# Attention visits in one piece from the fourth token block on, a third Gm buffer and a new order of issue

## The chip, the cores and the metric

The kernel runs on one core of a Trainium2 chip. The metric is the device time of one execution in microseconds (us). Before the change three runs took 610.43, 612.09 and 612.76 us, a median of 612.09. The profile is of one further execution, which took 611.65 us.

## The reference

The input passes through a decaying linear attention and then through two feed-forward layers of the same shape. Reduced to what matters:

```python
# attention: 4 batches, 8 heads, 768 steps, head size 32, state 16
cum = cumsum(log(clip(a, 1e-6, 1)))                  # within a chunk
M = (C @ B.T) * exp(cum_i - cum_j) * causal          # per head
y = M @ x + (C @ state) * exp(cum)
state = exp(cum_end) * state + (B * exp(cum_end - cum)).T @ x
x = y as 3072 tokens of 256
# layer 1, weights 256 x 2048 and 2048 x 256
h = x @ w_in;  g = h / (1 + exp(-h));  x = g @ w_out
# layer 2, the same shapes
h = x @ w_in;  g = P(h) / (Q(h) + 1e-6);  x = g @ w_out
# P of third degree; Q = 1 + |b0||h| + |b1|h^2
```

## The kernel before

The tokens are cut into 24 blocks of 128, six to a batch. For every block n the attention takes these steps. A DMA brings the block's x, B and C (`tok`, L561), and from block 3 on another brings decay factors (`Ee`, L579). GpSimd builds the masked decays `Gm` by four selects (L590) and scales B (L607). VectorE or GpSimd multiplies C with factors (L613), ScalarE or VectorE spreads it over pairs of heads (L618, L620), GpSimd scales it once more (L629). From block 9 on a copy of C and B is split into a high and a low part (`cf`, L647 and L651). TensorE makes C times B (tile `att`, input `tok` or `cf`); VectorE multiplies it with Gm into two tiles `M` (L700). TensorE then makes the output (from `M`, and from the state `S`) and the state's increment (`att<-tok`, 128 x 64), and VectorE masks and adds the increment (`um` L788, `S` L792). ScalarE writes the output rounded (`y1h`, L802), VectorE the rest (`y1l`, L805). The TensorE work of a block is its **visit**.

Both layers go through the 2048 hidden units in 16 slices f of 128. An **in-product** (tile `h`, in layer 2 also `b`) is six matmuls: high weight times high x, high times low, low times high, twice. An **out-product** (tile `acc`) is six matmuls on `gh` and `gl`, the activation's rounded part (L844, L846) and the rest (L850). Between the two stands ScalarE's activation (L888 in layer 1). Layer 1 goes through seven groups of blocks, of 2, 2, 4, 4, 4, 4 and 4; in the first two the activation stays in PSUM, so the in-product two slices on needs the buffer that `gl` frees. Layer 2 goes through six groups of 512 tokens.

The weights come as 64-bit floats, 512 KB for each slice and layer (`wraw`, L472, three buffers). ScalarE expands the upper word (`wv`, L489), VectorE shifts (L495) and joins the lower word (L497), which frees the buffer. ScalarE rounds (L513), and VectorE or GpSimd makes the rest, the **split** (L517). Layer 2's weights are prepared during layer 1, stored to DRAM (L529), and reloaded into a slice's place (L539) once its last layer-1 out-product is done.

All DMAs are issued by SP, in a single order. The order on every engine comes from a planner: `Plan.run` takes, of the operations that can start soonest by its cost table, the one with the smallest key, and some operations have a choice of engine. The keys come from the numbers in `K` (L31 to L69). 23 **fillers** (`acc<-T`, matmuls on zeros whose result is not used) have the last key of all and fall where the planner finds TensorE free. The order is fixed when the kernel is built; on the chip each engine works through its own list and waits where an input is not there.

`ALONE` (L79) says for which blocks C times B, output and increment are three operations of the planner; later visits are one operation that makes C times B of the next block, then the output, then the increment of this one. Before, that holds for blocks 0 to 4. `ring("Gm", 2, ...)` (L310) gives Gm two buffers.

Of the kernel before, what the change touches and what calls it, by code (L numbers as in the profile page):

```python
# [14 lines left out]
P = 128  # L15
B, H, S, D, N = 4, 8, 768, 32, 16
# [12 lines left out]
HALVED = 0  # L29
TAIL_FLEX = 1  # L30
K = dict(  # L31
    t0=-18.163,
    step0=2.86,
    lag1=43.503,
    fo1=10.942,
    fo2=4472.323,
    fol=32.531,
    tab=-80.822,
    lead=168.696,
    kt=-12.237,  # L40
    kq=-77.043,
    kl=20.552,
    kg=62.898,
    ks=777.795,
    warm=23,
    warm0=5.147,
    warmstep=0.414,
    late=46.508,
    tab0=-2757.678,
    bulk=-58.119,  # L50
    d0=-14.734,
    gap0=36.588,
    d2=-19.542,
    d3=2.257,
    early2=9.278,
    early=24.026,
    w2a=-1512.003,
    w2b=-160.848,
    w1=-1.707,
    w1step=-31.741,  # L60
    w1load=3869.872,
    tokload=-233.083,
    ahead=17.68,
    eps=0.031,
    step2=168.582,
    dT=[-64.27, 36.68, -1.66, 34.6, -29.6, -174.18, 35.5, -3.13, -9.78, 138.44, -41.72, -26.53],
    dD=[-124.33, -53.44, 1.94, -60.08, -128.23, 35.27, -89.78, -84.57],
    dW=[28.05, -44.69, -91.49, 180.41, 166.11, 92.54, 19.47, 34.68, 21.96, 122.42, 25.71, 20.72, -50.06, -0.22, -24.39, 76.24],
)  # L69
SET_LN_EXP, SET_SILU = 6, 18  # L70

# [4 lines left out]
C_DIF, C_REF, C_PAR, C_MASK, C_CUM, C_CEND = 0, 128, 134, 136, 200, 840  # L76
SW = 2 * D
IN_PSUM = 2
ALONE = 5  # L79
PARTS = 9  # L80


# [28 lines left out]
class Plan:  # L111
# [9 lines left out]
    def add(self, choices, key, deps=(), new=(), use=(), wr=(), rd=(), cols=0, after=0.0, big=True, soft=False):  # L121
        op = Op(choices, key, list(deps), list(new), list(use), wr, rd, cols, after, big, soft)
        self.ops.append(op)
        return op
# [91 lines left out]
def ssd_moe_moe_kernel(ctx: ExitStack, tc: tile.TileContext, tok, la_in, consts, w1, w2, ab, outT):  # L216
# [17 lines left out]
    def ring(tag, n, cols, dt=F32, space="SB"):  # L234
        rings[tag] = (Ring(n), n, cols, space)
# [71 lines left out]
    ring("cum", 1, C_CEND - C_CUM)  # L307
    ring("lab", 2, P)
    ring("Ee", 4, P + R5)
    ring("Gm", 2, H * P)  # L310
    ring("M", 3, 512)
    ring("S", 2, SW)
    ring("um", 1, SW)
# [396 lines left out]
    def cb_alone(n):  # L710
        t, T, d, o_cx = at[n][0], at[n][1], at[n][2], at[n][5]
        cb, f_cb = cb_part(n)
        o_cb = add({"PE": (0.61, f_cb)}, T + 2 * d, o_cx, new=[cb], use=[t], wr=range(4), cols=4 * DM, big=False)
        masked(n, cb, o_cb)


    def visit(n):
# [30 lines left out]
        y_len = 0.55 + (0.33 if pv else 0)  # L748
        if n < ALONE:
            o_y = add({"PE": (y_len, f_y)}, T + 5 * d, y_deps, new=[yb], use=y_use, wr=[0, 1], cols=P, big=False)  # L750
            if us:
                o_u = add({"PE": (0.21, f_u)}, T + 4 * d, [o_bw], new=[ub], use=[t], wr=[2], big=False)
            if n + 1 < min(NTB, ALONE + 1):
                cb_alone(n + 1)
# [415 lines left out]
```

## Time and profile before

| | |
|---|---|
| median of three runs | 612.09 us |
| the profiled execution | 611.65 us |
| its span, first to last instruction | 609.9 us |
| mean granted TensorE clock | 0.985 |
| busy: TensorE, VectorE, ScalarE, GpSimd | 597.7, 441.9, 401.2, 375.8 us |
| bytes moved by DMA | 47.30 MB |

The profile counts an engine as busy while it works on an instruction; waits on semaphores are idle time, and each is put down to what ended it. PE is TensorE, PEld its weight load, DVE VectorE, ACT ScalarE, POOL GpSimd, SPq the issue of DMAs by SP. The granted clock is a share of 2.4 GHz. The start of a stretch is counted from the first instruction.

### The profile page before, as it was taken

How to read it: one execution, taken by the hardware profiler on the slowest of the kernel's cores; microseconds unless marked ns; L12 is line 12 of the kernel's file. 1: busy time of each engine (PE TensorE's matmuls, PEld its weight loads, DVE VectorE, ACT ScalarE, POOL GpSimd, SP SyncE). 2: the span in 40 equal slices, each digit the busy share in tenths (PEclk: the TensorE clock that was granted, in tenths of full speed). 3: DMA queues.
4: the chain of work that ended last, by engine and by line, in shares of the span. 5: the costliest groups of instructions: out<-in, count | busy, mean ns of one | idle time of the engine just before them, and what ended most of it. 6: DMA issues, size and time to landing. Idle time of an engine off the chain costs nothing.

```text
span 609.9 us, 9980 instructions
## 1 busy us (share of the span) xinstructions
PE 597.7 (98%) x3501; PEld 478.6 (78%) x3505; DVE 441.9 (72%) x740; ACT 401.2 (66%) x782; POOL 375.8 (62%) x493
## 2 busy tenths in 40 slices
PE   7799999999999999999999999999999999999997
PEld 4478798887777777777888888888888788878875
DVE  5799988665344435432313899999999999999994
ACT  5678777554333333322335898989988988898893
POOL 5878846205344444222201599899889889889984
PEclk8599999999999999999999999999999999999999
DMA  7765778751111000000036600000000000000000
GB/s 258 227 199 209 234 250 286 243 200 37 46 28 36 23 21 27 1 2 1 1 104 199 250 0 1 36 1 1 35 1 2 34 1 1 35 1 1 35 2 34
DMA packets 18314, 47.30 MB, mean 78 GB/s; under 512 B 2136, under 2 KB 5336, under 8 KB 18264
## 3 DMA queue, kind: packets, MB, share of 16 engines
q1 hardware_dynamic: 18264, 46.67, 23.1%
q8 instruction: 27, 0.44, 0.3%
q14 instruction: 23, 0.19, 0.1%
HBM read 34.99 MB, written 11.67 MB: 77 GB/s over the span
## 4 chain that ended last, share of the span: by engine, by line
PE 88%; DVE 4%; DMA 4%; ACT 2%; issue 1%; SPq 0%; DVEq 0%; ACTq 0%
PE acc L280 42%; PE h L280 35%; PE b L280 7%; PE att L280 4%; DMA wraw<-in_w_dram 3%; DMA Ee<-dre 1%; DVE wv L497 1%; DVE w L517 1%; ACT wv L489 1%; DVE M L700 1%; DVE wv L495 0%; DVE gl L850 0%; ACT w L513 0%; DVE tok L613 0%; DVE y1l L805 0%
## 5 line engine op out<-in xcount | busy, mean ns | idle before, releaser
L280 PE MATMUL h<-y1h,w 128*128 128x512 f32 (+1 forms) x700 | 229.4, 377 | 2.3 <-DVE gl L850 1.9
L280 PE MATMUL acc<-gh,w 128*128 128x512 f32 (+1 forms) x832 | 213.1, 377 | 0.2 <-ACT gh L844 0.2
L280 PEld LDWEIGHTS acc<-gh,w 128*128 128x128 f32 x832 | 149.4, 188 | 30.6 <-POOL gh L846 0.4
L280 PEld LDWEIGHTS h<-y1h,w 128*128 128x128 f32 x700 | 129.7, 189 | 31.9 <-DVE gl L850 3.0
L850 DVE TENSOR_TENSOR gl<-T,gh 128x512 fp32r<-128x512 f32 x79 | 57.4, 727 | 116.0 <-POOL gh L846 84.8
L280 PE MATMUL h<-y1l,w 128*128 128x512 f32 (+1 forms) x350 | 130.8, 374 | 0.0
L850 POOL TENSOR_TENSOR gl<-g,gh 128x512 fp32r<-128x512 f32 x95 | 123.1, 1300 | 11.5 <-ACT gh L844 4.5
L280 PE MATMUL acc<-gl,w 128*128 128x512 f32 (+1 forms) x416 | 123.8, 378 | 0.0
L846 POOL TENSOR_SCALAR gh<-T 128x512 fp32r<-128x512 f32 x54 | 33.9, 627 | 137.2 <-ACT T L888 106.7
L888 ACT ACTIVATE T<-h 128x512 f32<-128x512 f32 x80 | 47.7, 597 | 97.6 <-PE h L280 91.8
L280 PEld LDWEIGHTS acc<-gl,w 128*128 128x128 f32 x416 | 75.9, 188 | 16.1
L953 POOL TENSOR_SCALAR tok<-T,abt 128x512 f32<-128x512 f32 x96 | 74.7, 778 | 16.3 <-ACT T L945 13.1
L280 PEld LDWEIGHTS h<-y1l,w 128*128 128x128 f32 x350 | 66.4, 190 | 11.6 <-DVE y1l L805 0.2
L956 DVE SCALAR_TENSOR_TENSOR b<-T,absb,b 128x512 f32<-128x512 f32 x96 | 71.9, 749 | 2.9 <-ACT b L949 2.6
L965 ACT ACTIVATE b<-b,lnb 128x512 f32<-128x512 f32 x96 | 64.1, 667 | 14.6 <-DVE b L956 14.6
L974 DVE SCALAR_TENSOR_TENSOR g<-tok,abt,b 128x512 f32<-128x512 f32 x96 | 71.3, 742 | 2.3 <-POOL gl L850 1.3
L590 POOL TENSOR_SCALAR_AFFINE_SELECT Gm<-eG 128x256 f32<-128x256 f32 x96 | 52.4, 581 | 9.8 <-ACT eG L386 6.0
L968 ACT ACTIVATE b<-b 128x512 f32<-128x512 f32 x96 | 56.8, 592 | 0.3
L962 DVE SCALAR_TENSOR_TENSOR tok<-T,abt,h 128x512 f32<-128x512 f32 x63 | 46.8, 743 | 0.9
L280 PE MATMUL b<-y1h,w 128*128 128x512 f32 x132 | 46.4, 392 | 0.0
L959 DVE TENSOR_TENSOR h<-tok,h 128x512 f32<-128x512 f32 x63 | 43.2, 686 | 0.0
L949 ACT ACTIVATE b<-h,abt 128x512 f32<-128x512 f32 x63 | 42.0, 667 | 0.9 <-DVE g L974 0.5
(76 smaller groups left out, 687.6 us busy)
## 6 DMA issues: line engine op xcount, KB each, us to landing
wraw<-in_w_dram SPq DMA_DIRECT2D x32, 512.0 KB, 5.1
w2s<-wraw SPq DMA_DIRECT2D x16, 512.0 KB, 3.4
w<-w2s SPq DMA_DIRECT2D x16, 512.0 KB, 4.2
tok<-in_tok_dram SPq DMA_DIRECT2D x24, 320.0 KB, 3.2
out_dram<-Gm SPq DMA_DIRECT2D x12, 256.0 KB, 2.0
Ee<-dre SPq DMA_DIRECT2D x21, 66.5 KB
cum<-in_consts_dram SPq DMA_DIRECT2D x1, 320.0 KB, 3.1
dre<-Ee SPq DMA_DIRECT2D x2, 66.5 KB
```

Of the source, the lines that this page charges most:

```text
L280: PE.matmul(out, lhsT, rhs, start=start, stop=stop)
L590: POOL.affine_select(g4[:, :, p * SUB : (p + 1) * SUB], eG[:, p, n * H : (n + 1) * H].unsqueeze(2).broadcast_to([P, H, SUB]), pattern=[[0, ...
L850: eng.tensor_tensor(gl.t[:, 0:W], g.t[:, 0:W], gh.t[:, 0:W], op=ALU.subtract)
L888: ACT.activation(T.t[:, 0:W], h.t[:, 0:W], AF.Silu)
L949: ACT.activation(c.t[:, 0:W], h.t[:, 0:W], AF.Abs, scale=abt[:, 4:5])
L953: POOL.tensor_scalar(t1.t[:, 0:W], s.t[:, 0:W], abt[:, 3:4], abt[:, 1:2], op0=ALU.mult, op1=ALU.add)
L956: DVE.scalar_tensor_tensor(c.t[:, 0:W], s.t[:, 0:W], absb[:, 1:2], c.t[:, 0:W], op0=ALU.mult, op1=ALU.add)
L959: DVE.tensor_tensor(h.t[:, 0:W], t1.t[:, 0:W], h.t[:, 0:W], op=ALU.mult)
L962: DVE.scalar_tensor_tensor(t1.t[:, 0:W], s.t[:, 0:W], abt[:, 2:3], h.t[:, 0:W], op0=ALU.mult, op1=ALU.add)
L965: ACT.activation(c.t[:, 0:W], c.t[:, 0:W], AF.Ln, bias=lnb)
L968: ACT.activation(c.t[:, 0:W], c.t[:, 0:W], AF.Exp, scale=-1.0)
L974: DVE.scalar_tensor_tensor(g.t[:, 0:W], t1.t[:, 0:W], abt[:, 0:1], c.t[:, 0:W], op0=ALU.add, op1=ALU.mult)
```

## The change

Three things change: the limit from which a visit is one operation (5 to 3, so blocks 3 and 4 are visited in one piece too), Gm's buffers (2 to 3), and most of the numbers in `K`. Of these two lines are shown; they mean nothing by themselves and act through the order.

```diff
 K = dict(
...
-    ks=777.795,
+    ks=6362.302,
...
-    ahead=17.68,
+    ahead=33.795,
...
 IN_PSUM = 2
-ALONE = 5
+ALONE = 3
 PARTS = 9
...
     ring("Ee", 4, P + R5)
-    ring("Gm", 2, H * P)
+    ring("Gm", 3, H * P)
     ring("M", 3, 512)
```

The order is the same on every engine up to about 17 us. Of the work, the same instructions are there, apart from where a choice of engine comes out otherwise. Three places follow, where a name's number is that of its buffer: `tok_131`, `tok_161`, `tok_199` and `tok_256` are blocks 1, 2, 3 and 4.

TensorE, from the end of block 1's output to the first in-product of layer 1 (`h`); `acc_73<-T_91` is a filler. Before:

```order
L280 MATMUL att_80<-M_280,tok_131 32x128 x4
L280 MATMUL att_81<-tok_199 32x64 x4
L280 MATMUL att_80<-tok_161 128x256 x2
L280 MATMUL att_81<-tok_161 128x256 x2
L280 LDWEIGHTS T_91
L280 MATMUL acc_73<-T_91 128x512
L280 MATMUL att_81<-tok_256 32x64 x4
L280 LDWEIGHTS T_91
L280 MATMUL acc_73<-T_91 128x512
L280 MATMUL h_355<-y1h,w_18_172 128x256
```

Now:

```order
L280 MATMUL att_80<-M_280,tok_131 32x128 x4
L280 MATMUL att_80<-tok_161 128x256 x2
L280 MATMUL att_81<-tok_161 128x256 x2
L280 LDWEIGHTS T_91
L280 MATMUL acc_73<-T_91 128x512
L280 LDWEIGHTS T_91
L280 MATMUL acc_73<-T_91 128x512
L280 LDWEIGHTS T_91
L280 MATMUL acc_73<-T_91 128x512
L280 LDWEIGHTS T_91
L280 MATMUL acc_73<-T_91 128x512
L280 MATMUL h_350<-y1h,w_18_172 128x256
```

The increments of blocks 3 and 4 (`att_81<-tok_199`, `att_81<-tok_256`) have left this place for their visits, and four fillers stand where two were.

ScalarE, from the second output `y1h` on; `w_34` is the rounded weight of slice 4, `wv_386` and `wv_383` the expanded weight of slice 6, `tok_324` and `tok_325` block 5. Before:

```order
L513 ACTIVATE w_31_327<-wv_262 128x512
L513 ACTIVATE w_34_333<-wv_307 128x512
L802 ACTIVATE y1h<-att_80 128x2x128
L489 ACTIVATE wv_346<-wraw_309 128x512
L618 ACTIVATE tok_256<-tok_256,con 128x128 x2
L888 ACTIVATE h_355<-h_355 128x256
L844 ACTIVATE gh_382<-h_355 128x256
L489 ACTIVATE wv_386<-wraw_348 128x512
L618 ACTIVATE tok_324<-tok_324,con 128x128 x2
```

Now:

```order
L513 ACTIVATE w_31_328<-wv_262 128x512
L802 ACTIVATE y1h<-att_80 128x2x128
L513 ACTIVATE w_34_335<-wv_307 128x512
L489 ACTIVATE wv_342<-wraw_309 128x512
L618 ACTIVATE tok_256<-tok_256,con 128x128 x2
L888 ACTIVATE h_350<-h_350 128x256
L888 ACTIVATE h_366<-h_366 128x256
L489 ACTIVATE wv_383<-wraw_344 128x512
L844 ACTIVATE gh_400<-h_350 128x256
```

`y1h` has moved ahead of one rounding, and the first `gh` behind the expansion of weight 6.

VectorE, from the shift of weight 7 on (`wv_443` before, `wv_471` now) to weight 8 (`wv_488`, `wv_516`); `tok_459` is block 6, `w_46` the split of weight 8. Before:

```order
L495 TENSOR_SCALAR wv_443<-wv_443 128x512
L792 SCALAR_TENSOR_TENSOR S_457<-S_318,Ee_278,um_336 128x64
L497 SCALAR_TENSOR_TENSOR wv_443<-wraw_384,wv_443 128x512
L788 TENSOR_TENSOR um_469<-att_81,con 128x64
L700 TENSOR_TENSOR M_473<-att_81,Gm_289 128x512
L805 TENSOR_TENSOR y1l<-att_80,y1h 128x2x128
L850 TENSOR_TENSOR gl_485<-h_405,gh_446 128x256
L850 TENSOR_TENSOR gl_496<-h_448,gh_479 128x256
L495 TENSOR_SCALAR wv_488<-wv_488 128x512
L613 TENSOR_TENSOR tok_459<-tok_459,Ee_401 128x128
L497 SCALAR_TENSOR_TENSOR wv_488<-wraw_441,wv_488 128x512
```

Now:

```order
L495 TENSOR_SCALAR wv_471<-wv_471 128x512
L700 TENSOR_TENSOR M_490<-att_80,Gm_320 128x512
L805 TENSOR_TENSOR y1l<-att_80,y1h 128x2x128
L700 TENSOR_TENSOR M_503<-att_81,Gm_320 128x512
L788 TENSOR_TENSOR um_519<-att_81,con 128x64
L850 TENSOR_TENSOR gl_521<-h_479,gh_505 128x256
L495 TENSOR_SCALAR wv_516<-wv_516 128x512
L792 SCALAR_TENSOR_TENSOR S_547<-S_318,Ee_278,um_519 128x64
L497 SCALAR_TENSOR_TENSOR wv_516<-wraw_473,wv_516 128x512
L497 SCALAR_TENSOR_TENSOR wv_471<-wraw_398,wv_471 128x512
L517 TENSOR_TENSOR w_46_576<-wv_516,w_46_576 128x512
```

The L613 of block 6 has gone to GpSimd, the split of weight 8 has come from there, and weight 7 is joined behind weight 8. Over the whole start, up to the split of weight 15, the L613 of blocks 5 to 8 and 11 and the splits of weights 6, 11 and 12 go from VectorE to GpSimd; the L613 of blocks 9 and 10 and the splits of weights 3 and 8 come the other way.

On SP the tokens of blocks 6, 7, 9 and 10 now stand ahead of weights 8, 9, 12 and 13, which stood ahead of them. At the seam of the layers, TensorE's last layer-1 in-product was followed by nine out-products of layer 1 and three in-products of layer 2 before the first out-product of layer 2; now seven and three follow.

## Rows read from the trace of the kernel before

**Rows 1.** The page's busy us, share of the span and instructions of each engine.

```profile
PE 597.7 (98%) x3501; PEld 478.6 (78%) x3505; DVE 441.9 (72%) x740; ACT 401.2 (66%) x782; POOL 375.8 (62%) x493
```

**Rows 2.** Busy us of PE, PEld, DVE, ACT, POOL by stretch, clock, DMA, GB/s.

```profile
17.00:75.00 58.00, 53.04 (x585) 41.41 (x588) 51.83 (x110) 42.98 (x109) 46.43 (x70) 0.90 0.70 220
75.00:600.00 525.00, 524.95 (x2818) 424.49 (x2811) 378.60 (x608) 347.68 (x650) 318.19 (x401) 1.00 0.17 57
```

**Rows 3.** PE's waits from 17 to 75 us: total us, times, longest.

```profile
PE h L280 <- DVE gl L850: 1.9, 3, 1.3
```

**Rows 4.** The same view as rows 2, its columns too, two stretches.

```profile
17.00:30.00 13.00, 9.95 (x81) 6.01 (x82) 9.48 (x21) 7.84 (x17) 10.66 (x17) 0.56 0.83 248
30.00:66.40 36.40, 35.15 (x380) 28.61 (x382) 34.83 (x72) 28.31 (x74) 29.77 (x45) 1.00 0.68 219
```

**Rows 5.** PE's timeline: start us, us, operation, idle before it and releaser.

```profile
23.95 0.44 PE L280 MATMUL att<-tok 128*32 128x64 f32 x8 [1.68 <-issue]
...
24.98 0.58 PE L280 MATMUL h<-y1h,w 128*128 128x256 f32 x1
...
30.23 0.39 PE L280 MATMUL h<-y1h,w 128*128 128x256 f32 x1 [1.25 <-DVE gl L850]
...
34.59 1.03 PE L280 MATMUL acc<-T 128*128 128x512 bf16 x4
...
66.44 0.62 PE L280 MATMUL att<-cf 32*128 32x256 f32 x12
...
346.22 1.09 PE L280 MATMUL acc<-gh,w 128*128 128x512 f32 x4
```

**Rows 6.** POOL's timeline at the seam of the layers.

```profile
340.19 1.30 POOL L850 TENSOR_TENSOR gl<-g,gh 128x512 fp32r<-128x512 f32 x1 [1.75 <-ACT gh L844]
```

**Rows 7.** The chain that ended last, 160 to 200 us: start us, us, what.

```profile
164.97 1.58 PE h L280 x6
166.55 1.39 PE acc L280 x6
```

**Rows 8.** The page's DMA issues: count, KB each, median us to landing.

```profile
w<-w2s SPq DMA_DIRECT2D x16, 512.0 KB, 4.2
```

**Rows 9.** ACT's timeline from the table load on.

```profile
23.27 1.15 ACT L513 ACTIVATE w<-wv 128x512 fp32r<-128x512 f32 x2
24.54 0.38 ACT L802 ACTIVATE y1h<-att 128x256 fp32r<-128x256 f32 x1
...
27.89 0.38 ACT L844 ACTIVATE gh<-h 128x256 fp32r<-128x256 f32 x1
29.16 0.66 ACT L489 ACTIVATE wv<-wraw 128x512 f32<-128x512 f32 x1 [0.89 <-DMA wraw<-in_w_dram]
```

**Rows 10.** POOL's groups, 30 to 66 us: busy us, mean ns, idle before.

```profile
L590 POOL TENSOR_SCALAR_AFFINE_SELECT Gm<-eG 128x256 f32<-128x256 f32 x24 | 14.7, 648 | 1.0 <-DVE M L700 1.0
L517 POOL TENSOR_TENSOR w<-wv,w 128x512 fp32r<-128x512 f32 x5 | 6.4, 1287 | 3.8 <-ACT w L513 3.8
...
L613 POOL TENSOR_TENSOR tok<-tok,Ee 128x128 f32<-128x128 f32 x2 | 0.9, 458 | 0.0
```

**Rows 11.** DVE's timeline around its restart.

```profile
29.55 0.29 DVE L613 TENSOR_TENSOR tok<-tok,Ee 128x128 f32<-128x128 f32 x1 [1.33 <-DMA Ee<-dre]
29.75 0.42 DVE L850 TENSOR_TENSOR gl<-h,gh 128x256 fp32r<-128x256 f32 x1
```

**Rows 12.** DVE's groups, 30 to 66 us: busy us, mean ns, idle before.

```profile
L517 DVE TENSOR_TENSOR w<-wv,w 128x512 fp32r<-128x512 f32 x6 | 4.9, 822 | 0.2
...
L613 DVE TENSOR_TENSOR tok<-tok,Ee 128x128 f32<-128x128 f32 x4 | 1.8, 450 | 0.0
```

**Rows 13.** SP's waits from 20 to 48 us: total us, times, longest.

```profile
SPq L561 <- PE att L280: 12.5, 5, 4.3
```

**Rows 14.** SP's timeline: start us, us, operation.

```profile
38.41 0.39 SPq L472 DMA_DIRECT2D wraw<-in_w_dram  x1
```

**Rows 15.** Tile wv from 17 to 75 us: ns min/median/max, first and last start.

```profile
L497 DVE SCALAR_TENSOR_TENSOR wv<-wraw,wv x17: 674/686/911, 16.3 to 74.0; 128x512 uint32<-128x512 uint32 x17
```

More of the change, by code (lines that the diff above doesn't have):

```diff
@@ L31 @@
 K = dict(
[L32 to L43, printed above, removed]
-    ks=777.795,
+    t0=9.461,
+    step0=3.004,
+    lag1=9.728,
+    fo1=9.918,
+    fo2=27635.151,
+    fol=18.035,
+    tab=-14.298,
+    lead=568.204,
+    kt=-48.015,
+    kq=-83.957,
+    kl=90.293,
+    kg=-15.472,
+    ks=6362.302,
     warm=23,
@@ L47 @@
     warmstep=0.414,
[L48 to L62, printed above, removed]
-    ahead=17.68,
+    late=70.772,
+    tab0=-10521.121,
+    bulk=-2.025,
+    d0=-26.692,
+    gap0=53.224,
+    d2=-13.265,
+    d3=2.512,
+    early2=-3.754,
+    early=42.418,
+    w2a=-1375.943,
+    w2b=-393.999,
+    w1=4.849,
+    w1step=-29.404,
+    w1load=8376.506,
+    tokload=-574.698,
+    ahead=33.795,
     eps=0.031,
[L65 to L68, printed above, removed]
+    step2=395.633,
+    dT=[-79.44, 29.45, 26.86, 24.01, -61.84, -218.22, 31.39, 30.97, -15.11, 167.05, -18.93, 2.4],
+    dD=[-155.28, -55.55, 7.83, -56.16, -173.83, 31.63, -137.36, -67.24],
+    dW=[17.59, -23.12, -107.14, 165.42, 181.82, 35.12, -9.11, 22.84, 19.25, 90.69, 36.29, -13.7, -9.44, 29.35, -10.43, 92.75],
 )
```

## The prediction

> **What bounds the kernel now.** I read the page's busy shares first: TensorE is busy 98% of the span, VectorE 72%, GpSimd 62% [rows 1]. 98% says where a gain can't lie, so the next view is the busy time by stretch: from 75 to 600 us TensorE is busy 524.95 of 525 us at a granted clock of 1.00 [rows 2]. Reordering there moves nothing as long as TensorE stays fed. Up to 17 us every engine's order is the old one. What is left is 17 to 75 us, where TensorE is busy 53.04 of 58 us [rows 2]; the largest of its waits there is for `gl`, 1.9 us in three places [rows 3].
>
> That stretch divides again [rows 4]. From 17 to 30 us TensorE is idle 3.05 us and its granted clock is 0.56, most of it the lower level, 1.2 GHz. From 30 to 66.4 us the clock is 1.00 and TensorE idle 1.25 us; it also runs fillers that compute nothing, 1.03 us of them recorded from 34.59 us [rows 5]. VectorE is the late one: busy 34.83 of these 36.4 us [rows 4]. Two engines are nearly full at once, and a gain needs both to give way.
>
> **What does not count.** From the third in-product of layer 2 on, TensorE's order is unchanged. At the seam, the first `gl` of layer 2 is made on GpSimd from 340.19 us, for 1.30 us [rows 6], and TensorE takes it at 346.22 [rows 5]: 4.7 us to spare. Between the last layer-1 in-product and that point stood nine out-products and three in-products; now it is seven and three, two groups of 1.39 us fewer [rows 7], so 1.9 us are left. Cost 0; with that cover gone, up to 2.8 us. A reloaded weight lands a median of 4.2 us after issue [rows 8]; between its release and first use stand three groups (4.17 us), for the first weight as before, for the second where there were six: 0, at worst a few tenths. Gm's third buffer ends GpSimd's wait for `M`, 1.0 us from 30 to 66 us [rows 10], but nobody reads Gm as early as it is then made: 0. Visits 3 and 4 in one piece each save one passage between attention and layer products: six products take 1.58 us behind a visit and 1.39 elsewhere [rows 7]. TensorE waits nearby anyway, so of these 0.2 us I take 0.
>
> **The terms, in order of time.**
> 1. *First layer product.* ScalarE rounds two weights (23.27, 1.15 us) and only then writes `y1h` at 24.54 [rows 9]; the first in-product starts at 24.98 [rows 5]. The change puts `y1h` between the two roundings, some 0.6 us earlier. Who waits next? The third in-product needs a PSUM buffer that `gl` of the first one frees; it starts at 30.23 after 1.25 us of idle time [rows 5]. So the 0.6 us reaches nothing by itself: 0.
> 2. *The restart at 29 us.* Before, ScalarE does `gh` at 27.89, then waits for weight 6 until 29.16 [rows 9]; VectorE waits for the factors of block 5 until 29.55 and makes `gl` at 29.75 [rows 11]. Now `gh` stands behind the expansion of weight 6, which the same transfers bring at the same time: 29.16 + 0.66 gives 29.8, `gh` ends 0.3 later, and `gl` starts at about 30.15. VectorE and all that queues on it start **0.4 us later**; bounds 0 (the load comes sooner) and 0.7 (nothing of ScalarE's overlaps).
> 3. *VectorE's load.* Up to the split of weight 15, five L613 products and three weight splits (L517) leave VectorE for GpSimd; two and two come back. From 30 to 66 us an L613 means 450 ns there and an L517 822 ns [rows 12]: 3 x 0.45 + 0.82 = 2.2 us. Successive rows start some 0.07 us before the last one's end, so **2.0 us less**; bounds 0 (waits take all of it) and 2.2.
> 4. *Weights behind it.* SP now sends tokens 6, 7, 9 and 10 ahead of weights that stood before them. Token loads wait for a visit to free their buffer, 12.5 us in five places [rows 13], and everything behind them on SP waits too. And VectorE finishes weight 7, whose buffer weight 10 needs, only after weight 8: 18 VectorE rows lead there from the restart at 30.15 us. At 34.83 us for 72 rows [rows 4] that is 8.7 us, so 38.9 with no wait counted, where weight 10 was sent at 38.41 [rows 14]. It leaves 0.4 to 0.8 us later, and weights 12 and 13, behind tokens 9 and 10, some 2 us later. Bounds 0 and 1.9 us, the latter if TensorE has nothing else when it asks for weight 13. I take **0.4 us**, weight 10's delay near its lower end, as VectorE has other work for part of it.
>
> Sum: +0.4 - 2.0 + 0.4 = **-1.2 us**. TensorE can give it, out of 1.25 us of idle time and 1.03 us of fillers. The profiled execution took 611.65 us, span 609.9 and 1.75 around it, so 610.45; it stands 0.44 us under the median of 612.09, and the forecast for the median is **610.9 us**: no change that can be told, as about 0.5% (3.06 us) is what a measurement of this kernel can tell from none.
>
> **A rule against it.** On VectorE the weights' shift-or L497 takes 674 ns at the least and 911 at the most [rows 15]; I put the long ones down to work on GpSimd beside them. If each of the eight operations that move to GpSimd held one VectorE operation by these 0.24 us, 1.9 of the 2.0 us would come back.
> The Trainium skill, "SBUF — State Buffer", section "SBUF: two separate sides", says that GpSimd and a VectorE operation with two SBUF inputs exclude each other over a shared port pair, the loser blocked for the winner's whole instruction. The trace agrees in kind, not in size: 0.24 us is far less than the 1287 ns of a whole GpSimd split [rows 10]. By the rule nearly all of term 3 is lost and the sum is near zero or above, the second rival below.
>
> **The rivals.**
> - *TensorE follows at once (faster).* Four fillers now run ahead of the first in-product, where 1.68 us of idle time, an attention product and two fillers were [rows 5]. If with them the clock is at 2.4 GHz when the products of 24.98 to 28.5 us start, these take half as long, up to 1.7 us less. With the 0.6 us of term 1 and the 1.25 us of idle time that is 3.5 us: 608.6. For it: VectorE's relief. Against: term 2's load, which comes at 29.16 however early TensorE is done.
> - *The port takes the relief back.* -1.2 + 1.9 = +0.7: 612.8.
> - *GpSimd becomes the bound (slower).* From 30 to 66.4 us it is busy 29.77 us [rows 4]. It gets five L613 at 458 ns and three splits at 1287 and loses two and one: 3.9 us more; Gm of block 11 (4 x 0.648 us [rows 10]) now comes before the last of this work: 36.3 of 36.4 us. Its waits for rounded weights, 3.8 us [rows 10], then have no room: if they stay, the work takes 3.7 us longer, or 1.1 if Gm 11 slides behind. It decides once GpSimd ends a split of weights 9 to 12 after TensorE could begin that product. I take 3.2, near the upper end, as its other waits are not counted: 615.3. Against: a new order fills some of these waits.
> - *It does nothing*: visits and Gm were never waited for, and the order only trades waits: 612.1, in the forecast's own range.
>
> **The numbers.** Forecast 0.50 (own range 609.4 to 612.3), TensorE follows 0.22, port 0.15, GpSimd 0.13. Faster by over 0.5% (under 609.0) takes the first rival and the edge of the forecast: 0.24. Slower by over 0.5% (above 615.15) takes most of the GpSimd case: 0.10. The rest is 0.66. The range leaves out the outer part of both, about 0.08 on each side: 607.6 to 614.8.
>
> **What would show it.** Right: in the changed profile `gl` of the first product at about 30.1 us, behind weight 6; VectorE's busy time from 30 to 66.4 us two us lower; one or two waits of TensorE over 1 us before 62 us, on `gl` or a weight; 100% from about 75 us on; the ninth visit (the first with `cf`), at 66.44 us before [rows 5], within 1.5 us of that. The sum is wrong if that visit comes before 64.5 us (first rival) or after 68.5 (GpSimd, at 95% from 30 us on), if L497 and L517 grow on VectorE (port), or if TensorE idles past 80 us, at the seam above all.

## The result and the profile after

Twenty executions of the changed kernel took 611.75 to 618.86 us, a median of **615.04 us**; twenty of the kernel before had a median of 611.1. The ratio is 1.006, with a 95% interval of 1.0048 to 1.0073: slower by 0.6%, an interval that stands clear of 1, where "no change" at 610.9 us was forecast.

The profiled execution is the slowest of the twenty: 618.86 us, span 617.1, mean clock 0.986. Its busy times, the answer to [rows 1]:

```profile
PE 601.8 (98%) x3505; PEld 482.5 (78%) x3505; DVE 444.1 (72%) x738; ACT 401.5 (65%) x782; POOL 375.7 (61%) x495
```

These shares tell nothing, as before. The stretches do; the columns are those of [rows 4]:

```profile
30.00:66.40 36.40, 32.25 (x364) 26.08 (x361) 32.62 (x64) 25.66 (x67) 31.47 (x47) 0.96 0.63 207
66.40:75.00 8.60, 8.60 (x88) 8.08 (x87) 5.60 (x13) 6.08 (x17) 1.73 (x4) 0.76 0.20 69
75.00:110.00 35.00, 32.21 (x327) 29.05 (x326) 27.31 (x60) 25.10 (x64) 17.59 (x32) 1.00 0.78 256
```

VectorE's busy time from 30 to 66.4 us is 2.2 us lower (32.62 against 34.83 [rows 4]). That is the number forecast, but this execution runs late, and only 64 of VectorE's rows fall between these times, where 72 did. TensorE is busy 2.9 us less there, 2.8 us short of full between 75 and 110 us, and in between, where it is 100% busy, its granted clock is 0.76. TensorE's timeline names the places (idle time before the row and its releaser in brackets):

```profile
59.53 0.50 PE L280 MATMUL h<-y1h,w 128*128 128x256 f32 x2 [0.85 <-POOL w L517]
...
63.14 0.50 PE L280 MATMUL h<-y1h,w 128*128 128x256 f32 x2 [1.48 <-DVE w L517]
...
64.71 0.55 PE L280 MATMUL h<-y1h,w 128*128 128x256 f32 x1 [0.76 <-DVE gl L850]
...
67.41 1.05 PE L280 MATMUL acc<-gh,w 128*128 128x256 f32 x4
...
71.73 0.62 PE L280 MATMUL att<-cf 32*128 32x256 f32 x12
...
105.64 0.50 PE L280 MATMUL h<-y1h,w 128*128 128x512 f32 x1 [1.95 <-DVE gl L850]
```

The waits at 59.53 and 63.14 are for the splits of weights 12 and 13. The one at 64.71, before in-product 14, is for the `gl` of slice 12, which frees the PSUM buffer and stands on VectorE behind the split of weight 14. Behind them four matmuls of an out-product take 1.05 us, which is the lower level of the clock, 1.2 GHz. The ninth visit starts at 71.73, 5.3 us later than in [rows 5].

### The profile page after: what moved, and what is told of

Read it like the earlier page. It is cut to its first block, busy times and chain, and to the rows that moved or that the text cites. A ratio compares the mean times of both kernels' runs of the same rounds, so it can differ in the third digit from the quotient of the medians.

```text
span 617.1 us, 9967 instructions
## 1 busy us (share of the span) xinstructions
PE 601.8 (98%) x3505; PEld 482.5 (78%) x3505; DVE 444.1 (72%) x738; ACT 401.5 (65%) x782; POOL 375.7 (61%) x495
## 4 chain that ended last, share of the span: by engine, by line
PE 87%; DMA 5%; DVE 4%; ACT 2%; issue 1%; SPq 0%; DVEq 0%
PE acc L280 41%; PE h L280 34%; PE b L280 7%; PE att L280 4%; DMA wraw<-in_w_dram 3%; DVE wv L497 1%; DMA tok<-in_tok_dram 1%; DVE M L700 1%; DMA Ee<-dre 1%; DVE gl L850 1%; DMA cum<-in_consts_dram 1%; ACT wv L489 1%; DVE wv L495 0%; ACT h L888 0%; DVE y1l L805 0%
## 5 line engine op out<-in xcount | busy, mean ns | idle before, releaser
L280 PE MATMUL h<-y1h,w 128*128 128x512 f32 (+1 forms) x700 | 232.3, 379 | 7.2 <-DVE gl L850 4.4
L888 ACT ACTIVATE T<-h 128x512 f32<-128x512 f32 x80 | 47.7, 597 | 106.8 <-PE h L280 106.6
L590 POOL TENSOR_SCALAR_AFFINE_SELECT Gm<-eG 128x256 f32<-128x256 f32 x96 | 53.4, 590 | 10.0 <-ACT eG L386 6.8
L945 ACT ACTIVATE T<-h 128x512 f32<-128x512 f32 x63 | 38.1, 604 | 6.9 <-PE h L280 5.8
```

Source lines behind the costliest of these rows:

```text
L280: PE.matmul(out, lhsT, rhs, start=start, stop=stop)
L590: POOL.affine_select(g4[:, :, p * SUB : (p + 1) * SUB], eG[:, p, n * H : (n + 1) * H].unsqueeze(2).broadcast_to([P, H, SUB]), pattern=[[0, ...
L888: ACT.activation(T.t[:, 0:W], h.t[:, 0:W], AF.Silu)
L945: ACT.activation(s.t[:, 0:W], h.t[:, 0:W], AF.Square)
```

## The experiments

All runs but e0, e4, e7, e8 and e10 take the changed kernel and edit the planner's order by a list of pairs; of a pair (a, b), step a goes right ahead of step b on its own engine, and nothing else moves. The pairs are written here with names where the kernels have the planner's running numbers.

```diff
-    for op in plan.run():
-        fn = op.choices[op.eng][1]
-        fn()
+    for op in reorder(plan.run(), MOVES):
+        op.choices[op.eng][1]()
```

Names in the lists: `wload`, `wexp`, `bits0`, `bits1`, `whi`, `wlo` are a weight's load, expansion, shift, join, rounding and split (with L2 for the second layer's); `tok`, `ce` (L613), `cx` (L618), `gm` (L590), `ph` and `pl` (L647, L651), `m` (L700), `um` and `s` (L788, L792), `xl` (`y1l`) are steps of the block whose number follows; `silu`, `ghi`, `glo` those of a group and slice.

To set profiles side by side, one length is used: from the start of the third in-product (30.23 us in [rows 5]) to the start of the last out-product of the second group of blocks (101.08 us before). What follows it takes 508.6 to 509.1 us in every one of these profiles, so nothing behind it counts. What lies ahead of it changes with the execution: that in-product starts between 28.88 us (e0) and 31.20 us (e5). And where visits 3 and 4 are in one piece, the length holds their two increments, some 0.23 us each, which before stand ahead of it. The measure of no loss for these versions is therefore e8, the kernel before with nothing but the visits changed: 71.37 us. Each length is that of one profile.

| run | median us | ratio to before (95%) | that length, us |
|---|---|---|---|
| before | 611.1 | | 70.85 |
| changed | 615.04 | 1.0060 (1.0048 to 1.0073) | 77.70 |
| e0, changed again | 614.25 | 1.0042 (1.0022 to 1.0063) | 72.66 |
| e1, loads | 613.74 | 1.0040 (1.0025 to 1.0055) | 72.44 |
| e2, split 13 | 616.97 | 1.0086 (1.0068 to 1.0104) | 75.50 |
| e4, fillers | 613.06 | 1.0026 (1.0013 to 1.0038) | 73.57 |
| e5, visit 7 late | 618.58 | 1.0110 (1.0084 to 1.0137) | 76.68 |
| e6 | 619.80 | 1.0127 (1.0105 to 1.0149) | 79.93 |
| e9 | 620.49 | 1.0146 (1.0118 to 1.0174) | 78.44 |
| e11 | 613.69 | 1.0035 (1.0018 to 1.0052) | 72.78 |
| e12 | 612.68 | 1.0021 (1.0004 to 1.0038) | 71.69 |
| e13 | 612.41 | 1.0014 (1.0001 to 1.0027) | 71.22 |
| e14 | 611.98 | 1.0010 (0.9998 to 1.0022) | 71.39 |
| e7, before + Gm | 611.41 | 0.9992 (0.9979 to 1.0005) | 70.97 |
| e8, before + visits | 612.22 | 1.0010 (0.9997 to 1.0023) | 71.37 |
| e10, before - fillers | 610.92 | 0.9998 (0.9984 to 1.0012) | 70.81 |

### The changed kernel again (e0)

> The changed kernel again, unaltered. The theory (weights 12 to 15 come late, TensorE waits for them at 59 to 65 us, and its clock then stays at the lower level until about 70 us) expects 614 to 616 us, TensorE idle for 2.5 to 3.5 us between 58 and 66 us, and a granted clock of 0.7 to 0.8 in the stretch 66.4 to 75 us again. The rival, that the profiled execution of 618.86 us was merely an unlucky one, expects a profile near 615 us whose clock stays up in that stretch and whose loss lies elsewhere.

Measured: 611.86 to 617.2 us. This profile is of an execution of 611.91 us, near the fastest, and it separates two things. TensorE's timeline has the waits before in-products 13 and 14 again, to 0.1 us (the second is put down to ScalarE's `gh`, done long before; `gl` ends at 61.22), and the products behind them are not slow:

```profile
59.80 0.50 PE L280 MATMUL h<-y1h,w 128*128 128x256 f32 x2 [1.48 <-DVE w L517]
...
61.37 0.36 PE L280 MATMUL h<-y1h,w 128*128 128x256 f32 x1 [0.83 <-ACT gh L844]
...
62.86 0.64 PE L280 MATMUL acc<-gh,w 128*128 128x256 f32 x4
...
66.59 0.62 PE L280 MATMUL att<-cf 32*128 32x256 f32 x12
```

```profile
30.00:66.40 36.40, 32.70 (x363) 26.96 (x362) 34.12 (x68) 27.64 (x72) 31.63 (x48) 1.00 0.61 203
66.40:75.00 8.60, 7.93 (x95) 7.11 (x93) 7.31 (x18) 7.13 (x20) 5.11 (x8) 1.00 0.75 241
```

In the windows the clock stays at 1.00. So the waits belong to the kernel, and the fall of the clock behind them to some executions. The wait for weight 12 is absent too. Both theories of the expectation were half right.

Three parts make up the 7 us between the two executions. The length begins 1.9 us later in the slower one (30.80 against 28.88 us). Up to in-product 13 it takes 1.4 us more, 0.85 of them the wait for weight 12. From there to its end it is 43.7 us in e0 and 47.3 in the slower execution, 3.6 us more. Half of these, 1.8 us, lie between in-product 14 and the ninth visit, where the products are slow. Nearly all of the other half is the wait at 105.64, 1.95 us where e0 has 0.32, and behind it stands the load of a weight that landed later, for which ScalarE waited (the slower execution first, then e0):

```profile
103.79 0.66 ACT L489 ACTIVATE wv<-wraw 128x512 f32<-128x512 f32 x1 [3.15 <-DMA wraw<-in_w_dram]
```

```profile
96.84 0.66 ACT L489 ACTIVATE wv<-wraw 128x512 f32<-128x512 f32 x1 [1.51 <-DMA wraw<-in_w_dram]
```

No run ties this load to the clock.

Why is the split of weight 13 late? VectorE's timeline in this execution:

```profile
54.41 0.40 DVE L805 TENSOR_TENSOR y1l<-att,y1h 128x256 fp32r<-128x256 f32 x1
54.73 1.27 DVE L700 TENSOR_TENSOR M<-att,Gm 128x512 f32<-128x512 f32 x2
55.93 0.41 DVE L850 TENSOR_TENSOR gl<-h,gh 128x256 fp32r<-128x256 f32 x1
56.26 0.84 DVE L497 SCALAR_TENSOR_TENSOR wv<-wraw,wv 128x512 uint32<-128x512 uint32 x1
57.03 0.66 DVE L495 TENSOR_SCALAR wv<-wv 128x512 uint32<-128x512 uint32 x1
57.61 0.43 DVE L792 SCALAR_TENSOR_TENSOR S<-S,Ee,um 128x64 f32<-128x64 f32 x1
57.97 0.94 DVE L497 SCALAR_TENSOR_TENSOR wv<-wraw,wv 128x512 uint32<-128x512 uint32 x1
58.83 2.05 DVE L517 TENSOR_TENSOR w<-wv,w 128x512 fp32r<-128x512 f32 x2
```

and in the kernel before:

```profile
55.82 0.67 DVE L497 SCALAR_TENSOR_TENSOR wv<-wraw,wv 128x512 uint32<-128x512 uint32 x1
56.42 1.74 DVE L517 TENSOR_TENSOR w<-wv,w 128x512 fp32r<-128x512 f32 x2
58.09 0.41 DVE L805 TENSOR_TENSOR y1l<-att,y1h 128x256 fp32r<-128x256 f32 x1
58.42 0.21 DVE L788 TENSOR_TENSOR um<-att,con 128x64 f32<-128x64 f32 x1
58.55 0.68 DVE L700 TENSOR_TENSOR M<-att,Gm 128x512 f32<-128x512 f32 x1
...
59.48 0.27 DVE L792 SCALAR_TENSOR_TENSOR S<-S,Ee,um 128x64 f32<-128x64 f32 x1
```

Before, weight 13 is joined and split (the second of the two L517) ahead of `y1l`, the masked products and the state that belong to visits 7 and 8. Now these, and the shift and join of weight 14, stand ahead of its split. VectorE has no idle time in these rows: it is not idle, it does the work of a later visit first.

### The loads (e1) and the split (e2)

```diff
+e1: (wload12, tok9), (wload13, tok10), (wload15, tok11)
+e2: (ghi0.10, ph10.0), (silu0.10, ghi0.10), (ph9.1, silu0.10), (whi12, cx10), (whi13, wexp14),
+    (bits1_12, ce10), (bits1_13, xl7), (wlo13, bits0_14)
```

> Only the DMA queue's order is altered: the loads of weights 12, 13 and 15 are issued ahead of those of tokens 9, 10 and 11. If the tokens ahead of the weights on the queue are what makes the weights late (the place that the prediction named), the waits at 59 to 65 us go, the clock stays up and the time is 611 to 612.5 us. If the buffers of the raw weights set the loads (weight 12's is free only at 45.1 us, when the shift and join of weight 9 end, and weight 13's at 49.3 us), the loads gain 1 us at most and the time is within 1 us of the changed kernel's 615.

Measured: 613.74 us, and the waits are e0's (1.9 us in two places for L517, the longest 1.5). The tokens on SP, to which the prediction's term 4 gave the delay, are not the cause.

> Only ScalarE's and VectorE's orders between 53 and 63 us are altered: the steps of token 10 go behind the expansion of weights 10 to 12, the join of weight 13 ahead of visit 7's, its rounding ahead of the expansion of weight 14 and its split ahead of the shift of weight 14. If these two waits (ScalarE idle 53.1 to 54.9 us for token 10, the split of weight 13 behind the join of weight 14) make TensorE wait, its idle time between 58 and 66 us falls from 3.3 us to below 1.5 us and the time is 611 to 613 us. If the loads or GpSimd's split of weight 12 set the pace, TensorE waits just as long at weight 12 or 13 and the time is 614 to 616 us.

Measured: slower, 616.97 us. TensorE's wait for weight 13 is gone, and one of 2.98 us has come before in-product 14, at 63.69: the `gl` of slice 12, for which it waits, still stands behind the split of weight 14. The two masked products still stood ahead. The clock is at the lower level behind that wait (0.91 from 66.4 to 75 us). Neither alternative had expected a loss.

### Fillers (e4, e10)

```diff
     for op in plan.run():
+        for _ in range(FILL.get(op, 0)):
+            f_warm()
```

Here FILL is 7 for in-product 13 and 3 for in-product 14; e10 leaves out the five fillers named in its expectation.

> Seven filler products are put ahead of in-product 13 and three ahead of in-product 14; nothing comes earlier by it, the weights included. If the lower clock after the wait costs time by itself (six products that took 8.0 us from 63.1 to 71.1 us where 0.88 us each at the higher clock would have made 5.3 us), the clock stays at 2.4 GHz and the time falls by 1.5 to 2.7 us, to 612.3 to 613.5. If only the lateness of the weights counts and what follows has slack for the slower products, it is 615 again, or more by up to 1 us where the fillers get in the way.

Measured: 613.06 us, 612.01 to 615.2. In its profile, too, GpSimd's split of weight 12 came 0.85 us late, as in the slowest execution; but the clock from 66.4 to 75 us is 1.00, and the length is 73.57 us against 77.70. The clock is also 1.00 in e0 and e1, which have no fillers there, so one profile doesn't show that the fillers kept it up. In medians the gain of 1.2 us over e0 lies within the two intervals, so it is likely and not shown.

> The kernel before without the five filler products that stand behind in-product 13, where TensorE waits for weights too (59.6 to 60.7 us). Nothing comes later by it. If fillers in that wait are what keeps the clock of the kernel before at its upper level, its clock now falls after 60 us in some executions, the spread of its times widens from 610 to 613 us to 610 to 616 us, and the median rises by 0.5 to 2.5 us. If the clock doesn't depend on them, the time is that of the kernel before within 0.3 us.

Measured: 610.92 us, 609.87 to 612.94. The kernel before doesn't need these fillers: without them it waits 0.65 us there and keeps its clock.

### Visit 7's steps behind the weights (e5, e6, e9, e11)

```diff
+e5: (um7, glo0.14), (xl7, glo0.14), (m8.0, glo0.14), (m8.1, glo0.14), (s7, glo0.14), (bits1_13, glo0.11)
+e9: (bits1_13, glo0.11), (um7, glo0.14), (xl7, glo0.14), (m8.0, wlo15), (m8.1, bits0_0L2), (s7, bits0_0L2),
+    (pl9.0, bits0_14), (pl9.1, wlo14), (whi15, cx11), (ce11, gm11)
-e9 to e11: (um7, glo0.14), (s7, bits0_0L2), (pl9.1, wlo14)
+e9 to e11: (um7, wlo14), (s7, wlo14), (pl9.1, bits0_0L2)
```

> Only VectorE's order is altered: five steps of visits 7 and 8 (the two masked products of block 8, the bmask product and the state of visit 7, its low part of y1), 2.4 us of work that nothing needs before 66 us, go behind the join of weight 15, and the join of weight 13 ahead of the low part of slice 11. The theory is now that VectorE, which does not idle from 50 us on, sets the pace, and that its order brings weights 13 and 14 late: their splits come 1 to 2 us earlier, TensorE's idle time between 57 and 66 us falls from 2.7 us (the repeat) to 1.5 us or less, and the time to 612 to 613.3 us, with fewer executions over 615. If something else sets the splits of 13 and 14 (the loads, ScalarE's roundings), the idle time stays and so does the time, 614 to 615 us.

Measured: 618.58 us. Weights 13 and 14 were in time, TensorE waiting 0.80 us once between 57 and 65 us, as expected. Weight 15 was not:

```profile
69.67 0.58 PE L280 MATMUL h<-y1h,w 128*128 128x256 f32 x1 [3.40 <-ACT w L513]
```

```profile
68.41 0.69 ACT L618 ACTIVATE tok<-tok,con 128x128 f32<-128x128 f32 x2 [4.51 <-POOL tok L613]
69.01 0.61 ACT L513 ACTIVATE w<-wv 128x512 fp32r<-128x512 f32 x1
```

```profile
65.26 1.64 POOL L590 TENSOR_SCALAR_AFFINE_SELECT Gm<-eG 128x256 f32<-128x256 f32 x4 [5.87 <-DVE M L700]
```

Read backwards: TensorE waits for the rounding of weight 15, which stands on ScalarE behind token 11's step, which waits for GpSimd's L613, which stands behind the Gm of block 11, which waits for a buffer until the masked products of block 8, the ones put off, are done. "Nothing needs them before 66 us" was wrong: nothing reads their results, but their buffers are needed. The clock fell as well: it is 0.61 from 66.4 to 75 us, so the 3.4 us are not the whole price.

The next run, e6, has the pairs of e5, of e1 and the first three of the section after this one.

> The order of the previous run, the weights' loads ahead of the tokens', and two small waits taken out: the low part of slice 4 ahead of visit 4's bmask product (TensorE waits 0.84 us for it before in-product 6), and the high and low parts of block 1's slice 1 ahead of the rounding of the next layer's weight 1 and of the masked products of block 9 (0.67 us). If these waits are what the change cost, the time is 610.5 to 612 us, level with the kernel before. If they move into others, it is 613 to 615.

Measured: 619.8 us, e5's chain again (3.4 us) and a wait of 1.59 us before in-product 11.

> The run e5 with its new wait taken out. There weights 13 and 14 came in time, but weight 15's rounding stood on ScalarE behind the expansion of token 11, which waited for GpSimd's L590 of block 11 and this for the masked products of block 8 that the run had put off: 3.4 us. Now the rounding of weight 15 stands ahead of token 11's step, GpSimd's step of token 11 ahead of its L590, the split of weight 15 between the two masked products, and block 9's low parts in VectorE's gaps. If VectorE's order between 53 and 66 us is what the change lost by, TensorE waits for less than 1.5 us between 57 and 72 us and the time is 611 to 613 us. If any order of these steps only moves the wait, it is 614 us or more.

Measured: 620.49 us. The second of the same kind: visit 7's state, late, held the factor tile of block 7 that the load of block 11's factors needs. VectorE ends the state at 64.29 us, and SP sends that load at 64.32. GpSimd's step behind the load, ScalarE's largest wait from 57 to 75 us, then TensorE's:

```profile
67.63 0.46 POOL L613 TENSOR_TENSOR tok<-tok,Ee 128x128 f32<-128x128 f32 x1 [10.59 <-DMA Ee<-dre]
```

```profile
ACT tok L618 <- POOL tok L613: 5.8, 1, 5.8
```

```profile
PE h L280 <- DVE gl L850: 6.4, 1, 6.4
```

> As the run e9, but visit 7's state (VectorE L788 and L792) is put ahead of the split of weight 14 instead of behind the low part of slice 14. In e9 that state, late, kept its factor tile (Ee) busy; the load of block 11's factors, GpSimd's step and ScalarE's expansion of token 11 waited one after another, and the high part of slice 15 behind them: 6.4 us. If that was all, TensorE waits for less than 2 us between 57 and 75 us, its clock stays up, and the time is 611 to 613 us. If VectorE's order cannot be altered there without another wait, it is 614 us or more again.

Measured: 613.69 us. With the state back the waits for weights are 0.6 us in two places, and 1.55 us have moved on to the first group's slice 15 at 69 us. The time is between the two expectations and can't be told from e0's.

### The waits behind (e12 to e14)

```diff
+e11 to e12: (glo0.4, um4), (ghi1.1, whi1L2), (glo1.1, m9.0)
+e12 to e13: (ghi0.15, whi0L2), (silu1.0, whi0L2), (ghi1.0, whi0L2), (glo0.15, bits1_0L2), (glo1.0, wlo0L2)
+e13 to e14: (xl1, m2.0)
```

> As e11, with the low part of slice 4 ahead of visit 4's bmask product (TensorE's wait of 0.84 us before in-product 6) and the high and low parts of block 1's slice 1 ahead of the rounding of the next layer's weight 1 and of the masked products of block 9 (a wait of 0.67 us). If these two waits are on the path, 0.5 to 1.5 us less than e11, 610 to 612 us; if TensorE only waits later for the same weights, the time is e11's.

> As e12, and the high and low parts of slice 15 and of block 1's slice 0 ahead of the expansion, rounding and split of the next layer's weight 0, behind which they stand on ScalarE and VectorE while TensorE waits 1.56 us for their PSUM bank (at 69 us). If orders on VectorE and ScalarE alone hold what is left of the loss, this takes 1 to 1.5 us off e12: 611 to 611.8 us, level with the kernel before. If the waits are only moved on, it is e12's 612 to 613 us.

> As e13, and visit 1's low part of y1 ahead of the first masked product of block 2, behind which TensorE waits for it 0.74 us after its first product (at 25 us). If the start is on the path, 0.4 to 0.7 us less than e13, 610.3 to 611.3 us; the prediction priced what the first products gain at 0, because TensorE meets the weights later anyway: by that it is e13's time.

Measured: 612.68, 612.41 and 611.98 us. Each step alone is below what can be told. Of the 1.1 us between the lengths of e11 and e12 a part can be the clock's: behind the same wait at 69 us it is 0.80 from 66.4 to 75 us in e11's profile and 1.00 in e12's. Together, from the changed kernel's 1.0060 (and e0's 1.0042) over e11's 1.0035, they come to 1.0010, whose interval holds 1. By the length, e14 (71.39 us) is level with e8 (71.37). The spread closes too: e14's highest time is 613.15 us, where the changed kernel reaches 618.86. e14's waits of TensorE from 40 to 75 us are

```profile
PE h L280 <- ACT h L888: 0.7, 1, 0.7
PE h L280 <- DVE w L517: 0.6, 2, 0.4
PE h L280 <- DVE gl L850: 0.5, 1, 0.5
```

e14 keeps single visits, three Gm buffers and the searched order up to 53 us but for two steps. No version measured beats the kernel before by more than its uncertainty.

### The two named parts alone (e7, e8)

```diff
     ring("Gm", 2, H * P)
+    rings["Gm"] = (rings["Gm"][0], 3, H * P, "SB")
```
```diff
-ALONE = 5
+ALONE = 3
```

The first is e7, where the planner still counts two buffers, so that the order stays. The second is e8, with the order of before written out.

> The kernel before with its own order in every engine, and three buffers for Gm instead of two: nothing but the waits for a Gm buffer goes. The prediction priced this part at 0: 611 to 612 us, within 0.2% of the kernel before. The rival, that GpSimd runs ahead with its four L590 instructions and takes the shared port from VectorE at a worse moment, expects 612.5 to 614 us.

> The kernel before with its own order and two Gm buffers, but visits 3 and 4 made single steps on TensorE (the state's product of blocks 3 and 4 no longer ahead of the first in-products, VectorE's four steps behind them accordingly). The prediction priced this part at 0: 611 to 612 us. The rival, that a single visit holds TensorE until its last input is there and so costs by itself, expects a new wait of over 0.5 us at visit 3 or 4 and 612.5 us or more.

Measured: 611.41 us (0.9992) and 612.22 (1.0010); both intervals hold 1. In e7 GpSimd's wait for `M`, 1.0 us in [rows 10], is gone and nothing comes of it. In e8 TensorE has no wait at all from 33 to 48 us, where visits 3 and 4 lie. So, as far as parts tried one by one can tell, the loss is the order's.

## Why the prediction was wrong

- **The stretch was right.** Everything that changed lies ahead of the end of the second group; behind it every profile takes the same time. The seam of the layers and Gm's third buffer, both priced at 0, cost nothing; single visits cost nothing that could be told.
- **The failing step is term 4**, +0.4 us with an upper bound of 1.9 "if TensorE has nothing else when it asks for weight 13". That case came. In e0, TensorE waits 1.48 us for weight 13 and 0.83 us before in-product 14, where e14's order has 0.4 and 0.7. The mechanism was wrong as well: the prediction looked at SP, but putting the loads first (e1) left the waits as they were. It read VectorE's new order at weights 7 and 8 and not at weights 13 and 14, where the masked products of block 8 stand ahead of a split that TensorE is about to ask for. How much of the loss these two waits are by themselves isn't shown: with the waits for weights down to 0.6 us (e11) the time is still e0's, as 1.55 us have moved on, and only all the moves of e14 together bring it back.
- **Term 3 was a right count with a wrong use.** That the busy time fell by the 2.2 us counted in the slowest execution is chance, since fewer rows fall in the window there. In e0, with 68 rows for 72, two splits and two products are gone from it (the split of weight 3, which the count took off the relief, lies ahead of 30 us): 2.5 us by the means of [rows 12]. The busy time fell by 0.7, so most of the relief came back, as the port rival said, and TensorE was no faster for the rest. The groups from 30 to 66.4 us, before and in e0 (busy us, mean ns, idle before):

```profile
L497 DVE SCALAR_TENSOR_TENSOR wv<-wraw,wv 128x512 uint32<-128x512 uint32 x11 | 8.4, 761 | 0.0
...
L495 DVE TENSOR_SCALAR wv<-wv 128x512 uint32<-128x512 uint32 x11 | 6.2, 565 | 0.4 <-ACT wv L489 0.4
```

```profile
L497 DVE SCALAR_TENSOR_TENSOR wv<-wraw,wv 128x512 uint32<-128x512 uint32 x11 | 8.9, 813 | 0.0
...
L495 DVE TENSOR_SCALAR wv<-wv 128x512 uint32<-128x512 uint32 x11 | 6.7, 608 | 0.1
L517 DVE TENSOR_TENSOR w<-wv,w 128x512 fp32r<-128x512 f32 x4 | 3.8, 976 | 0.7 <-ACT w L513 0.7
```

  11 x 52 ns, 11 x 43 ns and 4 x 154 ns (822 in [rows 12]) are 1.7 us, close to the 1.9 that the prediction took for this rival. GpSimd's part shows in single rows: from 30 to 66.4 us in these two profiles and e14's, an L495 with GpSimd idle beside it takes 0.41 to 0.43 us, one with GpSimd at work throughout 0.43 to 0.70. It did not decide: in e14 L497 and L495 are as long (812 and 598 ns) and the time is that of before. The Trainium skill, "SBUF — State Buffer", section "SBUF: two separate sides", lets the loser of the shared ports wait for the winner's whole instruction; the lengthening agrees in kind, but no mean here comes near a whole split on GpSimd (1287 ns, [rows 10]). What the relief was worth depended on which step came first on VectorE, not on how many it had.
- **The clock was not in the sum.** The prediction let it fall only at the start. A wait of 1.5 us in the middle was followed by the lower level in one profile of the changed kernel and not in the other; where it was, 1.8 us followed up to the ninth visit. With the late load (1.6 us), the 1.4 us ahead of weight 13 and a start 1.9 us later, that makes 618.86 us where e0's profile has 611.91. How often the clock falls is open, since a time alone doesn't show it.
- **Terms 1 and 2** were small and of the right kind. The first `gl` starts at 29.84 us in the slowest execution (30.1 forecast) and at 28.40 in e0, where the granted clock from 17 to 30 us was 0.87 against 0.61. The early start of the first rival thus came in e0, whose third in-product stands 1.35 us ahead of that of before, and the length, 1.8 us longer, took it back; e14's step at 25 us moved the median by 0.4 us, less than can be told.
- **GpSimd as the bound** did not occur: it was late once, at weight 12, after waiting 1.71 us for ScalarE's rounding. That this rival's 615.3 us lies next to the measured 615.04 is chance. The ninth visit as a test gave the right verdict (71.73 us, past the 68.5 set) for the wrong cause; in e0 it starts at 66.59, inside the forecast's 1.5 us, in a kernel that is slower all the same.

Left open: where the rest of the loss in the median lies, 2.7 us (e0) to 3.9, of which e0's length holds 1.3 over e8's and e1's 1.1, and how much of it the start or a fallen clock adds in other executions; the rest of 0.1% between e14 and the kernel before, if it is one (e8, with single visits alone, has the same 1.0010); what the fillers are worth in the changed kernel; and why token 10 landed so late in the slowest execution that ScalarE and VectorE waited for it. None of these was tried by itself.

## What to carry over

Where an order is new, look for the steps that a waiting engine asks for next, and read what stands ahead of them on the engine that makes them, through the whole stretch: a lower sum of busy time is worth nothing if a later visit's work goes first. Before a step is put off as not needed, list its buffers as well as its results: three of the runs here (e5, e6, e9) came out 4 to 6 us slower than e0, because a tile was held by a step whose result nobody wanted yet and the clock fell behind the wait. And take two profiles of a kernel whose times spread by 1%: the first showed waits, a late load and a fallen clock together, and only the second one told them apart.

## What was not expected of the hardware

The clock: the same two waits (1.48 and 0.8 us at in-products 13 and 14) were followed in one execution by products at 1.2 GHz, four matmuls in 1.05 us, and in another at 2.4 GHz, 0.64 us. A first guess would have been that a program which is the same in every execution meets its clock at the same places; here it doesn't, and a kernel that waits 2.3 us in its middle pays for it with the clock only now and then. e11 and e12 repeat it: behind the same wait of 1.55 us at 69 us the clock fell in the one profile and not in the other. Behind the waits of 2.98 to 6.39 us in e2, e5, e6 and e9 it fell in all four.
